# O's store and the modulation weights on GpSimd's DMA queue, and a reordered last stage, in a forward-and-backward memory transformer block

## The chip, the cores and the metric

The kernel runs on one core of a Trainium2 chip. The metric is the device time of one execution in microseconds (us); lower is better. The core has five engines with an instruction stream each: TensorE (PE; its weight loads are listed as PEld), VectorE (DVE), ScalarE (ACT), GpSimd (POOL) and SyncE (SP, which here only issues DMAs; its instructions appear as SPq). DMAs are issued by SP, GpSimd and in places ACT, and all of them are carried by the core's 16 DMA engines.

## The reference

The reference computes the output of a transformer block and the gradients of all its inputs. The block is a normalised attention with a recurrent memory, followed by a gated linear unit (GLU), each with shift, scale and gate rows that come from `silu(c) @ w_mod`. Cut to what matters here:

```python
mod = (_silu(c) @ w_mod).reshape(c.shape[0], 6, 1, -1)      # sa, ca, ga, sb, cb, gb
mem = mem0
for s in range(n_seg):                                       # 64 segments of 32 rows
    h = jnp.concatenate([mem, xs], axis=1)                   # 8 memory rows and 32 rows
    q, k, v = (einsum('btd,dhe->bhte', h, W) for W in (Wq, Wk, Wv))   # 32 heads of 128
    p = _softmax(where(mask, einsum('bhqe,bhke->bhqk', q, k) * scale, -1e9))
    o = einsum('bhqk,bhke->bhqe', p, v)
    o = einsum('bhte,hed->btd', o, Wo)
    mem = o[:, :M, :].copy()                                 # the next segment's memory
    outs.append(o[:, M:, :])
x = x + ga * attention(layernorm(x) * (1 + ca) + sa)
h = layernorm(x) * (1 + cb) + sb
x = x + gb * ((sigmoid(h @ w_gate) * (h @ w_up)) @ w_down)
# and the vjp of all this with grad_out
```

The sequence has 2048 rows of 512, so there are 64 segments; the eight memory rows make each segment depend on the one before. The backward pass needs V, P (the normalised softmax), O per head before the output projection, Q and K of every segment, so the forward pass stores them in DRAM.

## The kernel before, in words

`phase2` is the forward attention. Its loop `for s in range(NS)` has one turn per segment, called a stage here; `s4 = s % 4` is its position in a group of four segments, which share 128 rows. Heads are packed three to a 128-wide column block, so there are G = 11 blocks, in parts of four, four and three.

A stage does this. `proj` multiplies the segment's rows by Wk and Wq (L257), `v_chunk` by Wv (L677). `turns` transposes K and Q on TensorE. `st_exp` forms the scores (L900) and ACT their exponentials into `ET` (L902). `den` and `recip` (L906, L911) give the reciprocals of the row sums, `rden`. `pv` multiplies by V (L926); `ost` scales the product by `rden` into `Ost`, one part on DVE (L957), one on ACT (L954), one on DVE. `ott_first` and `ott_rest` transpose `Ost` into `OT`, `outproj` multiplies by Wo (L223), and `split_pair` with `sum_pair` give the stage's result, whose first eight columns ACT copies into the next stage's `hT` (L1133). In `split_pair` DVE writes `at_lo` (L232) once a stage, which makes a handy stage mark.

Besides that chain each stage moves data out. On SP, in this order: a DMA transpose of V into `VTr` (L1051), a DMA transpose of the exponentials `ET` into `Pst` (L1059), the store of `Ost` to `OSR` (L1089), the store of `OT` (L1127), every fourth stage or so six stores of the tail rows of K or Q, in some stages a load of modulation weights (`mod_rest`, L195), then for the stage before the stores of `VTr` and `Pst` to `VT` and `PS` (L1154, L1155), and the stores of K and Q (`rows_out`, L608 and L609). On GpSimd: the scaling of `Pst` by `rden` (L1152), three DMAs that bring the tail rows of V (L847), copies of the tails of K and Q (L65), the stores of attention rows to `AOA` (L811, L347), the copy `ao_tail` (L2379), and the copy of the next-but-one stage's input rows into `hT` (L563). The scaling of `Pst` and the stores of `VTr` and `Pst` are one closure, `norm`, which is put into `norms` at the end of a stage and called in the next.

`mod_rest` makes the later modulation rows in 16 pieces of 128 columns: `load` fetches the weights of a piece, `products` (L200) multiplies them one stage later.

The order of the work is written out by hand: `self.pin(i0)` at the end of `phase2` ties every engine's instructions of this phase to the order of the program text, and with them the order of the DMAs in each issuing engine's queue. The tile framework adds the waits. DMAs issued by SP take eight semaphores in turn, those issued by GpSimd another eight, so a DMA also waits until the one eight places before it has landed. `Ost` and `Pst` have one buffer each; `ET`, `OT`, `Vst` and the projected rows `RA` have two.

The last stage (s = 63) differs. It already does the GLU's norm for the first 128 rows (`first_tile_steps`; its variance is raised to a power on GpSimd, L776, and applied on DVE, L779). It transposes V and P on TensorE (`turn_v`, `turn_p`) and scales P by `rden` itself (`scale_p`, L946). It issues the loads of the next phase: rows for the GLU's second tile (`glu_load(1)`), `w_gate` (L996), `w_up` (L1061) and `w_down` (L1086), which take over the memory of Wk and Wv once these have been read.

`phase3` is the GLU, forward and backward, over 16 tiles of 128 rows. For the first tile PE multiplies by `w_gate` (L1333) and `w_up` (L1337), transposes `w_down` (L1242), and later needs `hhT`, a DMA transpose of the gated product `hh` (L1341) issued by SP (L1357, used in L1379). DVE prepares the second tile's rows meanwhile (L1266 to L1292).

Of the kernel before, what the change touches and what calls it, by code (L numbers as in the profile page):

```python
# [9 lines left out]
AF = mybir.ActivationFunctionType  # L10
ALU = mybir.AluOpType
# [29 lines left out]
class K:  # L41
# [145 lines left out]
    def mod_rest(self, psp, pool, k):  # L187

        nc, D, DC = self.nc, self.cfg.D, self.cfg.DC
        sl = slice(2 * D + 128 * k, 2 * D + 128 * k + 128)  # L190
        st = {}

        def load():
            st["w"] = pool.tile([128, DC, 128], BF16, name="wmod_r", bufs=1)
            nc.sync.dma_start(st["w"][:], self.io["w_mod"].rearrange("(cc p) n -> p cc n", p=128)[:, :, sl])  # L195

        def products():
            ps = psp.tile([128, 128], F32, name="mod_ps", tag="p")
            for n in range(2 * DC):
                nc.tensor.matmul(ps[0:32, :], lhsT=self.sc_keep[n % 2][:, n // 2, :], rhs=st["w"][:, n // 2, :],  # L200
                                 start=(n == 0), stop=(n == 2 * DC - 1))

            def put():
                row = pool.tile([1, 128], F32, name="modrow", bufs=1)
                nc.scalar.activation(row[:], ps[0:1, :], AF.Copy)
                nc.gpsimd.dma_start(self.MODROW[:, sl], row[:])

            return put

        return load, products  # L210
# [238 lines left out]
    def phase2(self):  # L449
        nc, tc, cfg, io = self.nc, self.tc, self.cfg, self.io  # L450
        D, DC, H, E, L, M, T, G, NS = cfg.D, cfg.DC, cfg.H, cfg.E, cfg.L, cfg.M, cfg.T, cfg.G, cfg.NS
        GW = 128
        NP = 3
        PG = 4
# [10 lines left out]
        with ExitStack() as ctx:  # L465
# [30 lines left out]
            Vsts = ptiles("Vst", 2)  # L496
            Ost = ptiles("Ost", 1)[0]
# [78 lines left out]
            def gl3(t):  # L576
                return t[:, :].rearrange("p (g x) -> p g x", x=GW)

            def x120(t, g):
                return t[:, g * 120:g * 120 + 128]  # L580
# [224 lines left out]
            norms = []  # L805
# [11 lines left out]
            turned_p = {}  # L817
# [39 lines left out]
            for s in range(NS):  # L857
# [13 lines left out]
                QT, KT, Vst, ET, OT = XT["q"], XT["k"], Vsts[s % 2], ETs[s % 2], OTs[s % 2]  # L871
                RA = RAs[s % 2]
                rden = sb2.tile([120, G], F32, name="rden")
# [21 lines left out]
                def st_exp(pi):  # L895
                    st_ps = masked.pop(pi)
                    n = min(PG, G - pi * PG)
                    for j in range(n):
                        g = pi * PG + j
                        nc.tensor.matmul(st_ps[:, j, 0:120], lhsT=x120(KT, g), rhs=QT[:, g * 120:g * 120 + 120],  # L900
                                         start=False, stop=True, skip_group_check=True)
                    nc.scalar.activation(part3(ET, pi)[:, 0:n, 0:120], st_ps[:, 0:n, 0:120], AF.Exp, scale=cfg.scale)  # L902
# [33 lines left out]
                def turn_p(pi):  # L936
                    n = min(PG, G - pi * PG)
                    ps = pst.tile([128, PG, GW], BF16, name="pt_ps", tag="st")
                    for j in range(n):
                        g = pi * PG + j  # L940
                        nc.tensor.transpose(ps[:, j, :], ET[:, g * GW:(g + 1) * GW], self.ident[:, :])
                    turned_p[pi] = ps

                def scale_p(pi):
                    n = min(PG, G - pi * PG)
                    nc.vector.tensor_tensor(Pst[0:120, pi * PG:pi * PG + n, :], turned_p[pi][0:120, 0:n, :],  # L946
                                            rden[:, pi * PG:pi * PG + n].unsqueeze(2).to_broadcast([120, n, 128]), op=ALU.mult)

                def ost(pi, or_ps, eng):
                    n = min(PG, G - pi * PG)  # L950
# [43 lines left out]
                if s == NS - 1:  # L994
                    self.glu_first = {1: self.glu_load(1, nc.sync)}
                    nc.gpsimd.dma_start(self.w_gate, io["B_w_gate"].rearrange("(c p) f -> p c f", p=128))  # L996
                    norms.pop()()
                if s == 0:
                    load_wo(3)
                    p1(P1_AHEAD, 0)  # L1000
# [35 lines left out]
                if s == NS - 1:  # L1036
                    v_chunk(s, 2)
                    first_tile[5]()
                st_exp(0)
                st_exp(1)  # L1040
                st_exp(2)
# [15 lines left out]
                if s < NS - 1:  # L1057
                    Pst = sb2.tile([128, G, 128], BF16, name="Pst", bufs=1)
                    nc.sync.dma_start(Pst[:], ET[:, :], transpose=True)  # L1059
                else:  # L1060
                    nc.gpsimd.dma_start(self.w_up, io["B_w_up"].rearrange("(c p) f -> p c f", p=128))  # L1061
                or1 = pv(1)
                ost(0, or0, "dve")
                ost(1, or1, "act")
# [18 lines left out]
                    self.pop_later()  # L1083
                self.pop_later()
                if s == NS - 1:
                    nc.gpsimd.dma_start(self.w_down, io["B_w_down"].rearrange("(fc p) d -> p fc d", p=128))  # L1086
                    for g0, t, w in ((0, RAs[0]["k"], 8), (8, RAs[0]["q"], G - 8)):
                        nc.sync.dma_start(self.VT[s, :, g0:g0 + w, :], t[:, 0:w * GW].rearrange("p (g x) -> p g x", x=GW))
                nc.sync.dma_start(self.OSR[s], gl3(Ost))  # L1089
                at_ps = outproj()  # L1090
                if s == NS - 1:
                    nc.sync.dma_start(self.OT[s], gl3(OT))
                    tail.collect(s4, [OT])
                    tail.begin(s - nseg_t + 1, [Wo])
                    first_tile[6]()
                    nc.scalar.activation(self.first_st[:, 11:12], self.first_st[:, 10:11], AF.Sigmoid)
                    parts = self.split_pair(sb2, at_ps, "at")
                    while tail.pieces:
                        tail.chunk()
                    tail.between = lambda: turn_p(0)  # L1100
                    tail.split()
                    first_tile[8]()
                    first_tile[7]()
                    ft = self.sum_pair(psp, parts, "at", "p")
                    self.store_rows(psp, sb2, ft, self.AOA[s + 1, 0:32, :], "at", "p")
                    self.pop_later()
                    self.pop_later()
                    turn_p(1)
                    self.pop_later()
                    for pi in (2, 0, 1):  # L1110
                        scale_p(pi)
                    break
                evac_turned()
                if s in first_tile[0]:
# [30 lines left out]
                    tail.collect(s4, [OT])  # L1145
                tail.split()
                self.store_rows(psp, sb2, ft, self.AOA[s + 1, 0:32, :], "at", "p")
                if s4 == nseg_t - 1:
                    tail.begin(s - nseg_t + 1, [Wo])

# [6 lines left out]
                if s < NS - 1:  # L1157
                    norms.append(norm)
            self.glu_first[0] = self.glu_load(0, nc.sync)
            nc.sync.dma_start(self.PS[NS - 1], Pst[:])  # L1160
            late_rows()
            self.pinned = self.pin(i0)

# [1357 lines left out]
```

## Time and profile before

| what | value |
|---|---|
| median of 3 runs | 2974.27 us |
| lowest and highest | 2969.84, 2976.05 us |
| profiled execution | 2976.26 us |
| its span | 2974.5 us |
| granted TensorE clock, mean | 0.998 |
| PE busy | 2913.0 us (98%) |
| DMA queue q1 (issued by SP and ACT) | 485.29 MB, 66.3% of the engines' time |
| DMA queue q0 (issued by GpSimd) | 148.63 MB, 15.9% |

The span runs from the first to the last instruction of the profiled execution; 1.76 us lie around it. A busy share is an average over phases: the forward loop takes the first 948 us, the GLU runs to about 1460 us, the attention's backward loop to about 2420 us, and weight gradients fill the rest. In the timeline a line gives start, length, engine, line of the kernel, operation and tiles, and in brackets the idle time before it with what ended it.

### The profile page before, as it was taken

Reading aid. Unit: us, or ns where it says so; the run is one execution under the profiler, and the core shown is the slowest. Engines: PE = TensorE matmul, PEld = TensorE weight load, DVE = VectorE, ACT = ScalarE, POOL = GpSimd, SP = SyncE. Lnnn points to the kernel's source line nnn. Section 1 sums busy time; section 2 is a strip of 40 time slices with the busy share of each in tenths; the row PEclk is TensorE's granted clock in tenths of the full one; section 3 lists DMA queues with packets and bytes.
Section 4 is the critical chain, followed back from the end, with each engine's and each line's share of the span. In section 5 each row is a group of like instructions: output and inputs, shape, how many; then the busy total and the mean of one; then the engine's idle time right before and its main releaser. Section 6 shows DMA issues by size and latency. Waiting matters only on the chain.

```text
span 2974.5 us, 105438 instructions
## 1 busy us (share of the span) xinstructions
PE 2913.0 (98%) x43838; PEld 1818.8 (61%) x43838; DVE 1625.0 (55%) x3689; ACT 1340.7 (45%) x3234; POOL 1231.7 (41%) x2487
## 2 busy tenths in 40 slices
PE   6999999999998999999999999999999999999999
PEld 3666666666665444445677776777777754445545
DVE  5565565665555788733456665666566632850011
ACT  3666666666665444312355555555555520110011
POOL 2555555545545222221344444444444432762111
PEclk9999999999999999999999999999999999999999
DMA  9889988998899899998699999999999997786565
GB/s 308 221 226 220 219 220 223 219 216 220 211 228 275 210 231 229 239 284 276 193 248 259 246 255 238 253 250 253 252 253 253 250 278 245 250 265 191 161 215 172
DMA packets 838066, 703.01 MB, mean 236 GB/s; under 512 B 537698, under 2 KB 710162, under 8 KB 836692
## 3 DMA queue, kind: packets, MB, share of 16 engines
q1 hardware_dynamic: 711972, 485.29, 66.3%
q0 software_dynamic: 54512, 148.63, 15.9%
q10 hardware_dynamic: 71104, 62.34, 6.5%
q8 instruction: 345, 5.65, 0.8%
q14 instruction: 133, 1.09, 0.1%
HBM read 294.99 MB, written 276.35 MB: 192 GB/s over the span
## 4 chain that ended last, share of the span: by engine, by line
PE 88%; DMA 4%; issue 3%; DVE 2%; ACT 1%; POOL 1%; SPq 0%; DVEq 0%; POOLq 0%; ACTq 0%
PE gps L2300 14%; PE pass_ps L257 14%; PE dh_ps L215 8%; PE g_ps L1923 5%; PE pass_ps L677 5%; PE gps5o L2315 4%; PE dhq_ps L223 4%; PE at_ps L223 4%; PE dh_tps L215 3%; PE gps L1583 3%; PE mm L1404 2%; PE turn_ps L890 2%; PE tps L1840 2%; PE st_ps L900 1%; PE mm L1364 1%
## 5 line engine op out<-in xcount | busy, mean ns | idle before, releaser
L2300 PE MATMUL gps<-rows,hrows 128*128 128x512 bf16 (+2 forms) x2160 | 415.5, 355 | 0.0
L2300 PEld LDWEIGHTS <-hrows 128*128 128x128 bf16 x2160 | 211.1, 98 | 204.5 <-issue 0.9
L1152 POOL TENSOR_TENSOR Pst<-Pst,rden 120x1408 bf16<-120x1408 bf16 x63 | 159.7, 2535 | 344.5 <-issue 209.0
L63 DVE CAST ot<-gps 128x512 bf16<-128x512 f32 (+3 forms) x76 | 48.1, 633 | 308.2 <-PE gps L2300 222.5
L1968 POOL COPY dOst<-RAd 96x512 bf16<-96x512 bf16 x128 | 75.1, 611 | 298.9 <-DVE RAd L63 298.7
L61 ACT ACTIVATE ot<-gps 128x512 bf16<-128x512 f32 (+3 forms) x75 | 41.2, 549 | 348.2 <-PE gps L2300 220.1
L677 PE MATMUL pass_ps<-Wv,hT 128*32 128x512 bf16 (+2 forms) x2304 | 186.8, 357 | 0.0
L2304 POOL DMA_DIRECT2D out_dram<-ot x104 | 78.6, 756 | 255.8 <-DVE ot L63 129.5
L257 PEld LDWEIGHTS <-hT 128*32 128x32 bf16 x4096 | 117.2, 97 | 95.9 <-issue 5.7
L63 DVE CAST Vst<-pass_ps 96x512 bf16<-96x512 f32 x128 | 87.3, 682 | 106.2 <-ACT RBv L61 102.7
L215 PE MATMUL dh_ps<-WvT,dVT 128*32 128x512 bf16 x2048 | 134.5, 383 | 1.7 <-DVE RBd L63 0.2
L223 PE MATMUL at_ps<-Wo,OT 128*32 128x256 bf16 x4096 | 128.1, 276 | 1.3 <-DMA Wo<-in_A_Wo_dram 0.9
L677 PE MATMUL pass_ps<-Wv,hb 128*32 128x512 bf16 (+2 forms) x636 | 126.5, 339 | 0.2
L257 PE MATMUL pass_ps<-Wk,hT 128*32 128x512 bf16 x2048 | 122.7, 380 | 2.1 <-POOL hT L563 1.1
L257 PE MATMUL pass_ps<-WoT,dyT 128*32 128x256 bf16 (+1 forms) x3072 | 122.8, 308 | 1.0 <-ACT dyT L2049 0.9
L257 PE MATMUL pass_ps<-Wq,hT 128*32 128x512 bf16 x2048 | 123.2, 379 | 0.3 <-DVE RBk L63 0.3
L223 PE MATMUL dhq_ps<-WqT,dQT 128*32 128x256 bf16 x4096 | 123.1, 273 | 0.2 <-issue 0.2
L215 PE MATMUL dh_ps<-WkT,dKT 128*32 128x512 bf16 x2048 | 122.3, 380 | 0.0
L2315 PE MATMUL gps5o<-WoT,rows 128*128 128x512 bf16 x560 | 121.0, 379 | 0.0
L223 PEld LDWEIGHTS <-dQT 128*32 128x32 bf16 x4096 | 109.9, 97 | 16.1 <-issue 0.4
L317 DVE TENSOR_TENSOR dST<-dh_ps,dST 128x512 bf16<-128x512 f32 x64 | 44.3, 692 | 130.3 <-ACT dST L316 130.3
L1910 DVE SCALAR_TENSOR_TENSOR dS<-dp_ps,Pst_l 128x480 bf16<-128x480 f32 (+1 forms) x192 | 106.2, 608 | 12.4 <-PE dp_ps L1908 6.7
(480 smaller groups left out, 7040.3 us busy)
## 6 DMA issues: line engine op xcount, KB each, us to landing
OSR<-Ost SPq DMA_DIRECT2D x64, 352.0 KB
OT<-OT SPq DMA_DIRECT2D x64, 352.0 KB
PS<-Pst SPq DMA_DIRECT2D x64, 352.0 KB
Pst_l<-PS SPq DMA_DIRECT2D x64, 352.0 KB
OT_l<-OT SPq DMA_DIRECT2D x64, 352.0 KB
DVR<-rows_x POOLq DMA_DIRECT2D x64, 352.0 KB, 6.0
DKR<-rows_x POOLq DMA_DIRECT2D x64, 352.0 KB, 5.7
DQR<-rows_x POOLq DMA_DIRECT2D x64, 352.0 KB, 3.5
```

Of the source, the lines that this page charges most:

```text
L63: return nc.vector.tensor_copy(out, in_)
L215: self.nc.tensor.matmul(ps[32 * j:32 * j + 32, :], lhsT=lhsT, rhs=w, start=(n < 4), stop=(n >= total - 4), tile_position=(0, 32 * j))
L223: nc.tensor.matmul(ps[32 * j:32 * j + 32, :], lhsT=x[k], rhs=w[k][:, 256 * d:256 * d + 256], start=(n == 0), stop=(n == total - 1), tile_p ...
L257: self.nc.tensor.matmul(ps[32 * j:32 * j + 32, :], lhsT=lhs(c), rhs=rhs, start=(c == 0), stop=(c == DC - 1), tile_position=(0, 32 * j))
L677: nc.tensor.matmul(ps[32 * j:32 * j + 32, o * E:(o + n) * E], lhsT=lhsT, rhs=wc[:, 3 * a + hl:3 * (a + n - 1) + hl + 1:3, :], start=(c == ...
L1152: nc.gpsimd.tensor_tensor(Pst[0:120, :, :], Pst[0:120, :, :], rden[:, :].unsqueeze(2).to_broadcast([120, G, 128]), op=ALU.mult)
L1583: nc.tensor.matmul(ps[:], lhsT=h2r[:, j, c * 128:(c + 1) * 128], rhs=xr[:, j, :], start=(j == 0), stop=(j == NT - 1))
L1910: nc.vector.scalar_tensor_tensor(out=part3(dS, pi)[:, :, 0:120], in0=ps[:, 0:n, 0:120], scalar=cfg.scale, in1=part3(Pst, pi)[:, :, 0:120], ...
L1923: nc.tensor.matmul(ps[:, j, 0:w], lhsT=lh[:, g * GW:(g + 1) * GW], rhs=rh[:, g * GW:g * GW + w], start=True, stop=True)
L2300: nc.tensor.matmul(ps[:, 0:ng * E], lhsT=hrows[:, tp_, c * 128:(c + 1) * 128], rhs=rows[:, tp_, 0:ng * E], start=(tp_ == 0), stop=(tp_ == ...
L2304: (nc.sync if i == len(todo) - 1 else nc.gpsimd).dma_start(outw[c * 128:(c + 1) * 128, h0:h0 + 3 * (ng - 1) + 1:3, :], ot[:, 0:ng * E].rea ...
L2315: nc.tensor.matmul(pss[gg][:], lhsT=rows[:, t, gg * E:(gg + 1) * E], rhs=dyrows[:, t, :], start=(n == 0), stop=(n == NTP - 1))
```

## The change

Four things are changed, all in `phase2` and `mod_rest`.

The store of `Ost` moves in stages 0 to 62 from SP's queue, ahead of the output projection, to GpSimd's queue, behind the calls that fold and store the stage's result. In stage 63 it stays on SP, and is now issued behind the projection's products in the program text.

The load of a piece of modulation weights moves from SP's queue to GpSimd's.

In stage 63 the closure `norm` of stage 62 moves from behind the projections of K to behind the norm's statistics, so that on GpSimd the scaling of P comes after the power L776. `w_up` is loaded right behind `w_gate`, and `w_down` ahead of `norm`.

In stage 63 `scale_p` runs on ACT, in eleven instructions of 128 columns in place of three on DVE, and writes into `Vst`, which is free by then, not into `Pst`. The three parts are spread over the end of the stage, and the store to `PS` reads `Vst`.

```diff
@@ mod_rest
-            nc.sync.dma_start(st["w"][:], self.io["w_mod"].rearrange("(cc p) n -> p cc n", p=128)[:, :, sl])
+            nc.gpsimd.dma_start(st["w"][:], self.io["w_mod"].rearrange("(cc p) n -> p cc n", p=128)[:, :, sl])
@@ scale_p
-                    n = min(PG, G - pi * PG)
-                    nc.vector.tensor_tensor(Pst[0:120, pi * PG:pi * PG + n, :], turned_p[pi][0:120, 0:n, :],
-                                            rden[:, pi * PG:pi * PG + n].unsqueeze(2).to_broadcast([120, n, 128]), op=ALU.mult)
+                    for j in range(min(PG, G - pi * PG)):
+                        g = pi * PG + j
+                        nc.scalar.activation(Vst[0:120, g * GW:(g + 1) * GW], turned_p[pi][0:120, j, :], AF.Copy,
+                                             scale=rden[:, g:g + 1])
@@ stage 63, behind the projections of K
                     nc.gpsimd.dma_start(self.w_gate, io["B_w_gate"].rearrange("(c p) f -> p c f", p=128))
-                    norms.pop()()
+                    nc.gpsimd.dma_start(self.w_up, io["B_w_up"].rearrange("(c p) f -> p c f", p=128))
@@ stage 63, behind the last part of V
                     first_tile[5]()
+                    nc.gpsimd.dma_start(self.w_down, io["B_w_down"].rearrange("(fc p) d -> p fc d", p=128))
+                    norms.pop()()
@@ between the products with V
-                else:
-                    nc.gpsimd.dma_start(self.w_up, io["B_w_up"].rearrange("(c p) f -> p c f", p=128))
@@ ahead of the output projection
                 if s == NS - 1:
-                    nc.gpsimd.dma_start(self.w_down, io["B_w_down"].rearrange("(fc p) d -> p fc d", p=128))
...
-                nc.sync.dma_start(self.OSR[s], gl3(Ost))
                 at_ps = outproj()
                 if s == NS - 1:
+                    nc.sync.dma_start(self.OSR[s], gl3(Ost))
                     nc.sync.dma_start(self.OT[s], gl3(OT))
...
                     parts = self.split_pair(sb2, at_ps, "at")
+                    scale_p(2)
...
                     self.pop_later()
+                    scale_p(0)
                     self.pop_later()
                     turn_p(1)
+                    scale_p(1)
                     self.pop_later()
-                    for pi in (2, 0, 1):
-                        scale_p(pi)
                     break
@@ end of the other stages
                 self.store_rows(psp, sb2, ft, self.AOA[s + 1, 0:32, :], "at", "p")
+                nc.gpsimd.dma_start(self.OSR[s], gl3(Ost))
@@ behind the loop
-            nc.sync.dma_start(self.PS[NS - 1], Pst[:])
+            nc.sync.dma_start(self.PS[NS - 1], gl3(Vsts[(NS - 1) % 2]))
```

## The prediction

> **What bounds the kernel now.** I read the page first: engine shares, the DMA row, the chain by line.
>
> ```profile
> span 2974.5 us, 105438 instructions
> PE 2913.0 (98%) x43838; PEld 1818.8 (61%) x43838; DVE 1625.0 (55%) x3689; ACT 1340.7 (45%) x3234; POOL 1231.7 (41%) x2487
> DMA  9889988998899899998699999999999997786565
> ...
> PE 88%; DMA 4%; issue 3%; DVE 2%; ACT 1%; POOL 1%; SPq 0%; DVEq 0%; POOLq 0%; ACTq 0%
> ```
>
> TensorE carries 88% of the chain, and the DMA engines are nine tenths busy through the first third (the loop over 64 stages, to about 948 us). The change touches only that loop and its end, so what it can win is the time in which PE waits there. The tile view of `Ost` says how much waits for its store to `OSR`:
>
> ```profile
> L1089 SPq DMA_DIRECT2D OSR<-Ost x64: 350/804/1962, 62.4 to 944.9; - x64
> ...
>   DMA OSR<-Ost: 10.7, 12
> ```
>
> `Ost` has one buffer, so the next stage's scaling (L957 on DVE, L954 on ACT) waits until the store has landed. Stage length I took as the distance between starts of `at_lo` (L232, once a stage): 13.96 to 14.03 us by stage position, and stages 1 to 62 together exceed that by 7.0 us. In the timeline DVE's first scaling starts 0.09 us after the reciprocal (L911) in an undisturbed stage; in stages 1, 4, 9, 13, 22, 28, 44, 47, 51, 52 it starts 0.74, 0.78, 0.41, 0.28, 0.44, 0.40, 0.29, 0.67, 0.53, 1.36 us after it: 5.9 less 10 x 0.09, so 5.0 us of the 7.0.
>
> The timeline of one stage shows where the two queues stand when `Ost` is ready (474.69 + 0.56 = 475.25):
>
> ```profile
> 480.13 0.39 POOL L2379 COPY ao_tail<-OT 128x264 bf16<-128x264 bf16 x1
> 480.48 0.26 POOL L563 COPY hT<-hx 128x96 bf16<-128x96 bf16 x1
> ...
> 483.89 0.53 SPq L1089 DMA_DIRECT2D OSR<-Ost  x1
> ```
>
> SP comes to the store at 483.89, behind two DMA transposes. GpSimd would come to it just ahead of the `hT` copy, at 480.48; the next `Ost` write is at 487.93. Last, the timeline of stage 63 and after, engine by engine:
>
> ```profile
> 936.74 2.53 POOL L1152 TENSOR_TENSOR Pst<-Pst,rden 120x1408 bf16<-120x1408 bf16 x1 [3.90 <-issue]
> 939.24 0.57 POOL L776 TENSOR_TENSOR st<-st 128x1 f32<-128x1 f32 x1
> ...
> 939.85 0.55 DVE L779 TENSOR_SCALAR RBv<-x,st 128x512 f32<-128x512 f32 x1 [2.36 <-POOL st L776]
> ...
> 942.15 1.14 ACT L954 ACTIVATE Ost<-or_ps,rden 120x128 bf16<-120x128 f32 x4 [2.89 <-DMA OSR<-Ost]
> ...
> 953.31 1.75 DVE L946 TENSOR_TENSOR Pst<-pt_ps,rden 120x384 bf16<-120x384 bf16 x3 [1.22 <-DMA PS<-Pst]
> ...
> 959.49 0.96 PE L1242 MATMUL tp<-ident,Wv 128*128 128x128 bf16 x14 [1.13 <-DMA Wv<-in_B_w_down_dram]
> ...
> 977.75 0.75 PE L1379 MATMUL mm<-Wv,hhT 128*128 128x512 bf16 x2 [3.08 <-DMA hhT<-hh]
> ```
>
> Stage 63 takes 18.95 us (929.15 to 948.11). Two things hold it at once: the power (L776) stands on GpSimd behind P's scaling (L1152), and stage 62's `OSR` store lands at 942.04. Then come three DMA-made waits.
>
> **The change part by part.** All sums are against the profiled execution, 2976.26 us (span 2974.5, 1.76 around it). The three runs' median is 2974.27, 2 us lower, which is as much as the waits vary from run to run.
>
> *O's store, 63 times, from SP to GpSimd.* SP loses 0.80 us a stage; OT, VT, PS and the K and Q stores behind it come earlier, but nothing on the path waits for those, so this counts nothing. GpSimd gains an issue of 0.57 us (the 352 KB store of `DVR` has that row). Behind it stand the `hT` copy (used a stage later), P's scaling, V's tail rows and the K and Q tails; cover is GpSimd's idle time before P's scaling, 324 us over 59 stages in the waits view. So the cost of the issue is nothing. What matters is whether the store lands before the next `Ost` write. From the start of each stage's `hT` copy to that write there are 6.83 us or more at the last position of each group of four, 7.45 to 7.54 typically at the first and third, 9.6 at the second; stages 22 and 44 are outliers with 5.53 and 4.61, where P came late. The landing of such a store from GpSimd is not in the trace for the forward loop. The nearest rows are the same size in the backward loop:
>
> ```profile
> DMA to landing us min/median/max: 2.8/3.5/4.9
> DMA to landing us min/median/max: 4.6/5.7/7.4
> DMA to landing us min/median/max: 4.7/6.0/8.3
> ```
>
> (`DQR`, `DKR`, `DVR`.) With one landing time for all 62 stages, the lateness adds up to 0 at 3.5, 0.4 at 5.0, 1.9 at 6.0, 9.5 at 7.3 and 32.5 at 8.0. I take 5.0, the mean of the three medians, since 128 KB stores from GpSimd in this very loop (`H1ROWS`) land in 4.3 and SP's own 352 KB store in stage 51 landed 4.5 after its issue (779.71 to 784.2). Result: -5.0 + 0.4 = -4.6 (bounds -5.0 and +27). [...]
>
> *Modulation weights, 16 loads, from SP to GpSimd.* Two loads come too late now: PE waits at L200 in stages 7 and 55, and periods 8 and 56 are 0.39 and 0.48 us long. Issued on GpSimd a few us sooner and used a stage later, both waits go: -0.9. The issue costs GpSimd 0.5 to 0.8 (`MODROW` 0.51; `w_gate`, with as many runs, 0.78), ahead of O's store at the third position, where 7.45 shrinks to about 6.7; still over 5.0, so nothing.
>
> *Last stage, the power ahead of P's scaling, stage 62's store sooner.* The variance is ready at 934.80; the power is done by 935.5 and DVE's L779 follows the V copy at 937.5. The copies of V and the reciprocal then end near 939.45, not 941.18. O's store of stage 62 goes out at 932.1 ahead of `w_gate` in the same queue and is there by 938 if it takes 5.0 to 6.0. `Ost` starts at 939.5, not 942.15: 2.65. PE's idle stretches at 939.4 to 942.9 mostly go, and with them the clock of 0.50 and 0.66 that the windows show at 944 to 948, where L223's 64 products took 3.46 instead of 1.94 us: up to 1.4 more. At `at_lo` stage 63 is then 4.0 shorter. P's scaling now ends about 942.3; behind it wait the store of `at_rb` and the `ao_tail` copy, needed by PE at 944.8: 1 us of slack.
>
> *GLU weights sooner, P of stage 63 on ACT.* The 4.0 meet the transfers:
>
> ```profile
> 934.00:936.00 2.00, 2.00 (x34) 1.26 (x31) 1.60 (x5) 1.19 (x3) 0.00 (x0) 1.00 0.97 291
> 942.00:944.00 2.00, 1.04 (x12) 0.69 (x12) 1.80 (x5) 1.14 (x4) 0.00 (x0) 0.99 0.95 234
> 954.00:956.00 2.00, 2.00 (x13) 1.05 (x11) 1.97 (x4) 1.48 (x3) 0.66 (x3) 1.00 1.04 408
> ```
>
> The last two columns are DMA share and GB/s: full from 930 to 960, with a dip at 942 to 944, when `w_gate` is in and `w_up` (issued 941.08, landed 11.7 later) only starts. Issued at 933 and 939, the weights leave no such gap; at some 270 KB a us (`w_gate`, 1.8 MB, went at that rate from 934 to 940), O's store and 5.5 MB end near 957, not 959.4. So PE's L1242 moves by 2 to 2.5, not 4.0. DVE loses 1.75 us and a 1.22 us wait, ACT gets 11 scalings of 0.285 (1.14 for four in L954): three in its 1.34 us of idleness before L316, eight in the 2.18 before the first sigmoid; 0.2 to 0.5 may stick out, which the wait for `w_up` covers. New wait: P of stage 63 lies in `Vst`, whose memory the first `hh` (L1341) takes over, so `hh` waits for that store. It went out at 956.86, `hh` ran at 963.68; with a landing of 4.4 to 10.1 (P's store of stage 62, issued 943.08, took the latter) this costs 0 to 3.3 after a shift of 2.5; I take 0, as the queue is emptier by then (0.76 share at 960 to 965). After that PE waits 3.08 for `hhT`, whose transpose SP issues at 969.60, 8.8 us after OT's landing released its queue (960.76). If SP's queue is released as much sooner as the weights land, the wait stays as it is; if not sooner at all, the gain shrinks to under 1; if 5 sooner, the wait goes too. Ends 0.5 and 5.1; I take 2.7, near the weights' shift.
>
> Sum: -4.6 - 0.9 - 2.7 = -8.2, so 2968.1, rounded 2968.0.
>
> **The rivals.**
>
> *O's store lands late (slower).* If behind the two transposes a store from GpSimd needs 8.0 us, 43 of 62 stages are stalled: 32.5 - 5.0 - 0.9 - 2.7 = +23.9, 3000. It decides from a landing of 7.3 on. For it: `DVR` reaches 8.3, and stage 62's store on SP took 9.7 beside `w_gate`. Against: no median above 6.0, and GpSimd's queue has only small stores at that moment.
>
> *The queue changes, the transfers do not (no change).* The engines are 0.9 busy whoever issues. If O's store pushes the transposes of P back by its own time, P's scaling, the next item on GpSimd, goes back too and with it the next store: the loop gives some 2, the tail 0.5, in all -2 to -4: 2972 to 2974. For it: P's scaling waits for its transpose in most stages, and two stages have little slack already. [...]
>
> *The tail opens fully.* SP's queue drained 5 us sooner, `hhT` no longer waited for: -5.1 in place of -2.7, with the loop at its best 2965, down to 2962.
>
> **How the numbers follow.** Forecast 0.50, open tail 0.10, no change 0.24, late store 0.16. A measurement of this kernel tells about 0.2%, 6 us, from no change, so the forecast (6.3 under the median) lies just beyond it: of its 0.50 I count 0.40 as faster. Faster 0.50, same 0.10 + 0.24 = 0.34, slower 0.16. The range runs from the open tail, 2962, to just past the median with one or two stages stalled more, 2979; it leaves out the late store and little else. The forecast's own range is 2964 to 2972.
>
> **What would show it.** Right: the lengths of stages 1 to 62 exceeding undisturbed ones by under 2 us in all, not 7.0; no wait for `OSR` over 1 us in all; no PE wait for `wmod_r`; stage 63 at 15 us; L776 before L1152 on GpSimd; `w_down`'s end near 957. Wrong: `OSR<-Ost` landing over 7 us after its issue on GpSimd; DVE and ACT waiting for it at the last position of every group; `hh` waiting for `PS<-Vst`; the wait for `hhT` grown to 5.

## The result, and the profile after

The changed kernel is slower. Its median is 3025.59 us against 2971.42 us for the kernel before, a ratio of the medians of 1.018. The comparison's own ratio is 1.0107, 95% interval [1.0079, 1.0135]; it counts only executions within 1.5% of the changed kernel's fastest, and since these spread from 2976 to 3046 us, most are left out of it, the profiled one too; `e2` below shows the same loss with none left out. The prediction was 2968.0 us, range 2962 to 2979. The profiled execution took 3029.94 us.

The page of the changed kernel, the lines that answer to the first fence of the prediction:

```profile
span 3028.2 us, 105299 instructions
PE 2932.9 (97%) x43838; PEld 1821.5 (60%) x43838; DVE 1628.0 (54%) x3686; ACT 1343.6 (44%) x3245; POOL 1286.9 (42%) x2566
DMA  9888888888899989998699999999999997786565
...
PE 65%; DMA 2%; issue 2%; DVE 1%; ACT 1%; POOL 0%; SPq 0%; DVEq 0%; POOLq 0%; ACTq 0%
```

TensorE does the same work, but is busy 19.9 us longer, and the span is 53.7 us longer. The chain is no help here: it could be followed back only to 877.5 us, so it covers little of the loop. The starts of `at_lo` do. The one of stage 62 has moved from 929.15 to 983.35, so the loop lost 54.2 us; from there to the end it is 2044.8 us against 2045.3. The loss is not spread evenly. By position in the group of four, the median stage is 13.96, 14.03, 16.36 and 15.47 us (before 13.98, 14.02, 13.96 and 14.01): the third is longer, and often the fourth.

What stands in the third position is shown by the tile view of `b_colsk`, the tile from which GpSimd copies the last rows of K (`kT`, L65) in every stage, and which ACT fills anew once in four stages:

```profile
L65 POOL COPY kT<-b_colsk x186: 187/230/812, 68.6 to 983.9; 128x192 bf16<-128x192 bf16 x62, 128x48 bf16<-128x48 bf16 x62, 128x16 bf16<-128x16 bf16 x62
L61 ACT ACTIVATE b_colsk<-turn_ps x15: 597/597/603, 83.4 to 924.9; 128x512 bf16<-128x512 bf16 x15
...
who waited for it (us, times):
...
  ACT b_colsk L61: 37.5, 13
```

ACT waited 37.5 us for GpSimd's copies, in 13 stages. The same line of the kernel before:

```profile
  ACT b_colsk L61: 1.0, 2
```

Stage 18, in the timeline of the changed kernel, SP, GpSimd, ACT and PE in turn (start, duration, and in brackets the idle time before it and what ended it):

```profile
311.60 1.85 SPq L1054 DMA_TRANSPOSE VTr<-Vst  x1
313.54 2.23 SPq L1062 DMA_TRANSPOSE Pst<-ET  x1
322.31 0.42 SPq L1156 DMA_DIRECT2D VT<-VTr  x1
322.92 1.95 SPq L1157 DMA_DIRECT2D PS<-Pst  x1
...
311.67 0.56 POOL L1149 DMA_DIRECT2D OSR<-Ost  x1
312.22 0.28 POOL L563 COPY hT<-hx 128x96 bf16<-128x96 bf16 x1
320.36 2.54 POOL L1154 TENSOR_TENSOR Pst<-Pst,rden 120x1408 bf16<-120x1408 bf16 x1 [7.87 <-DMA Pst<-ET]
324.42 0.65 POOL L65 COPY kT<-b_colsk 128x192 bf16<-128x192 bf16 x3
...
325.10 0.60 ACT L61 ACTIVATE b_colsk<-turn_ps 128x512 bf16<-128x512 bf16 x1 [3.46 <-POOL kT L65]
325.59 0.38 ACT L230 ACTIVATE at_hi<-at_ps 128x256 bf16<-128x256 f32 x1
...
326.02 0.27 PE L242 MATMUL at_ft<-foldsel,at_hi 128*128 128x32 bf16 x4 [2.56 <-ACT at_hi L230]
```

O's store is issued 0.07 us after the transpose of V starts on SP. P's transpose, issued at 313.54, lets P's scaling start only at 320.36; the copies `kT` stand behind the scaling, ACT's `b_colsk` behind the copies, and `at_hi`, for which TensorE waits, behind that. In the kernel before, P's scaling started 6.84 us after `at_lo` of stage 17 (302.37 less 295.53) in this stage; here 11.25 us after it (320.36 less 309.11), and the stage takes 16.96 us.

The fourth position is explained by the row of Wk's products in the page and by the granted clock. The row, before and after:

```profile
L257 PE MATMUL pass_ps<-Wk,hT 128*32 128x512 bf16 x2048 | 122.7, 380 | 2.1 <-POOL hT L563 1.1
...
L257 PE MATMUL pass_ps<-Wk,hT 128*32 128x512 bf16 x2048 | 135.0, 409 | 2.1 <-POOL hT L563 1.1
```

That is 12.3 us more for the same 2048 products, 409 ns each instead of 380. Windows of 1 us around the stall of stage 18 (window, length, busy time and instructions of PE, PEld, DVE, ACT and POOL, then granted clock, DMA share, GB/s):

```profile
323.00:324.00 1.00, 0.46 (x12) 0.00 (x0) 0.00 (x0) 0.00 (x0) 1.00 (x3) 1.00 0.94 345
324.00:325.00 1.00, 0.00 (x0) 0.00 (x0) 0.00 (x0) 0.00 (x0) 1.00 (x4) 1.00 0.61 169
327.00:328.00 1.00, 1.00 (x20) 0.56 (x16) 0.93 (x5) 1.00 (x4) 1.00 (x3) 0.50 0.70 217
328.00:329.00 1.00, 1.00 (x16) 0.46 (x12) 0.46 (x2) 0.31 (x2) 0.98 (x3) 0.50 0.80 203
329.00:330.00 1.00, 1.00 (x16) 0.33 (x12) 0.45 (x1) 0.00 (x0) 1.00 (x3) 0.50 1.17 125
330.00:331.00 1.00, 1.00 (x24) 0.44 (x20) 0.24 (x1) 0.25 (x1) 0.68 (x2) 0.98 1.18 161
```

After the idle stretch TensorE's granted clock is 0.81 in the window at 326, 0.50 in the three from 327 and 0.98 at 330. So 36.5 us of added waiting for `b_colsk` and 12.3 us of slower products make up 48.8 of the 54.2, as a rough account: a wait of ACT need not delay TensorE by as much.

The waits for O's store, which the change was expected to remove, have nearly doubled. The tile view of `Ost`, from which the prediction had 10.7 us in 12 waits of DVE and ACT together, now has:

```profile
  DMA OSR<-Ost: 20.2, 14
```

Of these 10.7 us are DVE's, in seven stages (4.5 in five before). The tile view of `OSR`, changed kernel:

```profile
L1149 POOL DMA_DIRECT2D OSR<-Ost x63: 542/557/607, 56.5 to 988.1; - x63
...
  DVE Ost L958: 10.7, 7
...
DMA to landing us min/median/max: 3.5/5.4/9.3
```

And the last stage (timeline of the changed kernel, GpSimd, then DVE, then PE):

```profile
990.72 0.57 POOL L776 TENSOR_TENSOR st<-st 128x1 f32<-128x1 f32 x1 [0.54 <-DVE st L775]
996.45 2.53 POOL L1154 TENSOR_TENSOR Pst<-Pst,rden 120x1408 bf16<-120x1408 bf16 x1 [0.81 <-issue]
...
997.41 2.13 DVE L783 SCALAR_TENSOR_TENSOR RBv<-ca_bc,RBv 128x512 f32<-128x512 f32 x1
...
1013.75 0.96 PE L1244 MATMUL tp<-ident,Wv 128*128 128x128 bf16 x14 [0.24 <-DMA Wv<-in_B_w_down_dram]
1032.66 0.60 PE L1381 MATMUL mm<-Wv,hhT 128*128 128x512 bf16 x2 [3.98 <-DMA hhT<-hh]
```

The power (L776) is ahead of the scaling, and stage 63 is 17.10 us long instead of 18.95. But `w_down` is used 30.4 us after `at_lo` of stage 62, as before (30.3), and the wait for `hhT` is 3.98 us, not 3.08.

### The profile page after: what moved, and what is told of

It reads as the page before. It is cut to its first block, busy times and chain, and to the rows that moved or that the text cites. A ratio compares the mean times of both kernels' runs of the same rounds, so it can differ in the third digit from the quotient of the medians.

```text
span 3028.2 us, 105299 instructions
## 1 busy us (share of the span) xinstructions
PE 2932.9 (97%) x43838; PEld 1821.5 (60%) x43838; DVE 1628.0 (54%) x3686; ACT 1343.6 (44%) x3245; POOL 1286.9 (42%) x2566
## 3 DMA queue, kind: packets, MB, share of 16 engines
q14 instruction: 132, 1.08, 0.1%
## 4 chain that ended last, share of the span: by engine, by line
PE 65%; DMA 2%; issue 2%; DVE 1%; ACT 1%; POOL 0%; SPq 0%; DVEq 0%; POOLq 0%; ACTq 0%
PE gps L2302 14%; PE dh_ps L215 8%; PE pass_ps L257 6%; PE g_ps L1925 5%; PE gps5o L2317 4%; PE dhq_ps L223 4%; PE mm L1406 3%; PE dh_tps L215 3%; PE gps L1585 2%; PE mm L1381 2%; PE mm L1366 2%; PE tps L1842 1%; PE mm L1335 1%; PE mm L1339 1%; PE gps L1484 1%
## 5 line engine op out<-in xcount | busy, mean ns | idle before, releaser
L1154 POOL TENSOR_TENSOR Pst<-Pst,rden 120x1408 bf16<-120x1408 bf16 x63 | 159.8, 2536 | 392.4 <-issue 284.3
L257 PE MATMUL pass_ps<-Wk,hT 128*32 128x512 bf16 x2048 | 135.0, 409 | 2.1 <-POOL hT L563 1.1
```

Of the source, the lines that this page charges most:

```text
L257: self.nc.tensor.matmul(ps[32 * j:32 * j + 32, :], lhsT=lhs(c), rhs=rhs, start=(c == 0), stop=(c == DC - 1), tile_position=(0, 32 * j))
L1154: nc.gpsimd.tensor_tensor(Pst[0:120, :, :], Pst[0:120, :, :], rden[:, :].unsqueeze(2).to_broadcast([120, G, 128]), op=ALU.mult)
```

## The theories

Theory A: P goes round a loop once a stage. SP issues the DMA transpose of P; when it has landed GpSimd scales P; when that is done SP issues P's store; behind it in SP's queue stand K's and Q's stores and the next two transposes, so the next transpose of P cannot be issued earlier. In the kernel before, O's store stood behind both transposes in the same queue. From GpSimd it is under way beside them, P lands later, and the loop becomes longer than a stage; what depends on GpSimd then falls behind until it stops the path. Theory B: GpSimd's own additional instructions delay its queue. Theory C: the rebuilt last stage costs the time.

The loop can be measured in each profiled execution: means over stages 2 to 61, worked out from the starts and ends in the timelines, in us. The last column says how long after `at_lo` P's scaling starts.

| kernel | P's transpose issued to scaling | scaling | to P's store | store to next transpose of P | sum | scaling after `at_lo` |
|---|---|---|---|---|---|---|
| before | 4.97 | 2.54 | 0.68 | 5.85 | 14.04 | 7.74 |
| after | 6.41 | 2.54 | 0.12 | 5.92 | 14.99 | 10.11 |
| `e1` store back on SP | 5.12 | 2.54 | 0.49 | 5.98 | 14.13 | 7.82 |
| `e2` store alone | 6.05 | 2.54 | 0.29 | 6.05 | 14.93 | 10.22 |
| `e6` idle instructions | 5.07 | 2.54 | 0.57 | 5.86 | 14.04 | 7.17 |
| `e9` half the store | 5.70 | 2.54 | 0.34 | 5.99 | 14.57 | 9.61 |
| `e10` store between | 4.96 | 2.54 | 0.37 | 6.78 | 14.64 | 9.99 |
| `e8` tails first | 6.26 | 2.54 | 0.32 | 5.78 | 14.89 | 12.60 |
| `e12` less scaling | 5.87 | 1.26 | 0.81 | 6.16 | 14.09 | 5.18 |
| `e11` after, P before V | 6.44 | 2.54 | 0.92 | 4.03 | 13.94 | 4.04 |
| `e13` before, P before V | 5.83 | 2.54 | 1.54 | 4.03 | 13.94 | 2.57 |
| `e14` `e13` and the store | 6.14 | 2.54 | 1.25 | 4.33 | 14.26 | 7.90 |

The sum is within 0.12 us of the mean stage, as it must be when both go in step (from the `at_lo` starts of stages 2 to 62, 14.09 before and 14.98 after), so the sum alone does not tell which of the two sets the pace. The column "to P's store" tells more: it holds SP's delay in coming to that store, and this is the slack. Before, it was 0.68 us a stage, 0.12 after. In the three kernels with P's transpose ahead of V's it is not all slack, because V's store stands ahead of P's on SP and waits there for V's transpose (46.0 us in 30 stages in `e13`).

## The experiments

### Which part: `e1` to `e4`

`e1_store_back`: the changed kernel, O's store returned to SP.

```
-                nc.gpsimd.dma_start(self.OSR[s], gl3(Ost))      # behind store_rows
+                nc.sync.dma_start(self.OSR[s], gl3(Ost))        # ahead of outproj()
```

> The changed kernel with O's store issued by SP again; the modulation weights and the last stage stay as changed. Theory A (in GpSimd's ring the store's transfer runs beside the two DMA transposes, they land later, and the loop transpose of P -> P's scaling on GpSimd -> store of P -> next transposes, about 14.0 us long before, becomes longer than a stage): the start of P's scaling returns from 15.0 us apart to 14.1, at_lo of stage 62 from 983 to below 931 us, and the time is 2964 to 2971 us. Theory B (GpSimd's own extra instructions, the modulation weights' loads among them, delay its queue): most of what came in the stages that load weights stays, 2975 to 2990 us. Theory C (the rebuilt last stage costs the time): no change to 3020 us or more.

2977.2 us, ratio to the kernel before 1.0005 [0.9995, 1.0015]. The loss is gone, and `b_colsk` waits 1.3 us in all. The level is a miss (2964 to 2971 was expected): the remaining two parts do not make the kernel faster than before.

`e2_store_alone`: the kernel before, with that one edit the other way round.

> The kernel before with O's store alone moved to GpSimd. Theory A: nearly the whole loss, 3015 to 3040 us, P's scaling 15.0 us apart. Theory C: as before, 2971 us. Theory B leaves room for less than theory A: 2990 to 3020 us.

3036.4 us, 1.0206 [1.0186, 1.0226]. One moved instruction brings the whole loss. ACT's wait (tile view of `b_colsk`, this kernel):

```profile
who waited for it (us, times):
  DVE b_colsk L63: 61.6, 15
  ACT b_colsk L61: 43.8, 15
```

`e3_weights_alone`: the kernel before with the modulation weights' loads on GpSimd.

```
-            nc.sync.dma_start(st["w"][:], self.io["w_mod"]...)
+            nc.gpsimd.dma_start(st["w"][:], self.io["w_mod"]...)
```

> The kernel before with the modulation weights' loads alone moved to GpSimd. Theory A: 2968 to 2973 us, no stage longer than before by more than 1 us. Theory B (GpSimd's queue is delayed by more issues): 2980 us or more, with the longer stages behind the loads at the third position of each group of four.

2981.4 us, 1.0025 [1.0013, 1.0038]. That is the level of theory B (2980 or more) and not of theory A, but without theory B's pattern: the third positions keep their normal length (13.96 us in the median). PE no longer waits for `wmod_r`, but stage 4 takes 18.91 us, 4.9 too long, and `Ost` waits 3.11 us for O's store there; no other stage exceeds its normal length by more than 1.6 us.

`e4_last_stage_alone`: the kernel before with the edits of stage 63 only (the power and the GLU weights ahead of P's scaling, P of stage 63 scaled by ACT into `Vst`).

> The kernel before with the edits of the last stage alone. The prediction's sum for this part is -2.7 us (bounds -0.5 and -5.1): 2968.7 us against 2971.4. Theory C: 3000 us or more.

2976.7 us, 1.0005 [0.9993, 1.0016]. Theory C falls, and the predicted -2.7 is not there. Stage 63 takes 19.15 us: with O's store still on SP, that of stage 62 holds it (timeline, DVE):

```profile
945.96 0.69 DVE L958 TENSOR_TENSOR Ost<-or_ps,rden 120x512 bf16<-120x512 f32 x1 [2.84 <-DMA OSR<-Ost]
```

### The issue or the transfer: `e6`, `e7`, `e9`, `e10`

`e6_idle_on_gpsimd`: the kernel before with idle instructions where the change issues the store.

```
                 self.store_rows(psp, sb2, ft, self.AOA[s + 1, 0:32, :], "at", "p")
+                for _ in range(2):
+                    nc.gpsimd.memset(idle_t[:], 0.0)
```

> The kernel before (O's store on SP) with two memsets of a scratch tile of 128x384 bf16 on GpSimd at the place where the change puts the store; a 128x264 copy there takes 0.39 us, so some 0.8 us in all, more than the store's issue of 0.56. Theory A (the transfer beside the transposes does it): 2970 to 2978 us, and b_colsk waits on ACT for the tail copies kT less than 4 us in all (1.0 before, 37.5 after the change). Theory B (GpSimd's queue is delayed by the instruction itself): 2995 us or more, with 15 us or more of that wait.

2975.1 us, 0.9997 [0.9984, 1.0009], and a wait for `b_colsk` of 2.1 us. The tile view shows what GpSimd was given in addition, 0.84 us a stage:

```profile
L1150 POOL MEMSET idle_t<- x126: 407/418/582, 56.4 to 935.3; 128x384 bf16 x126
```

Theory B falls.

`e7_store_act`: the kernel before, the store issued by ScalarE at its old place.

```
-                nc.sync.dma_start(self.OSR[s], gl3(Ost))
+                nc.scalar.dma_start(self.OSR[s], gl3(Ost))
```

> The kernel before with O's store issued by ScalarE at its old place in the program: the transfer leaves SP's queue and runs beside the two transposes, and GpSimd issues nothing more. Theory A: 3000 to 3040 us, P's scaling 14.6 us apart or more, b_colsk waits for kT's tail copies 25 us or more. Theory B: 2968 to 2980 us, that wait under 4 us.

3024.1 us, 1.0171 [1.0144, 1.0199]. The time and the loop (14.74 us) are as theory A has them, but the wait is not: 0.4 us for `kT`. The timeline of ACT shows another obstacle:

```profile
379.99 0.35 ACTq L1089 DMA_DIRECT2D OSR<-Ost  x1
380.39 0.60 ACT L61 ACTIVATE b_colsk<-turn_ps 128x512 bf16<-128x512 bf16 x1 [1.89 <-DMA VT<-VTr]
```

The store's issue on ACT waits until the store of V has landed, and that hangs on the same loop. So ACT is stopped by the issue itself, and this run does not separate the theories cleanly.

`e9_half_store`: the changed kernel, the store in two parts.

```
+                if s < NS - 1:
+                    nc.sync.dma_start(self.OSR[s, :, 6:G, :], gl3(Ost)[:, 6:G, :])
                 at_ps = outproj()
...
-                nc.gpsimd.dma_start(self.OSR[s], gl3(Ost))
+                nc.gpsimd.dma_start(self.OSR[s, :, 0:6, :], gl3(Ost)[:, 0:6, :])
```

> The changed kernel with O's store in two parts: six of the eleven column groups from GpSimd, five from SP at the old place. Theory A: about half of the loss, as the time that the transposes share is halved, 2980 to 3010 us, P's scaling 14.2 to 14.7 us apart. Theory B (the number of GpSimd's instructions counts, and it is the same as in the change): 3015 us or more.

3005.5 us, 1.0104 [1.0074, 1.0135]. With none, half or all of the store on GpSimd, P's transpose takes 4.97, 5.70 and 6.05 to 6.41 us to the scaling, and the loop 14.04, 14.57 and 14.93 to 14.99: it is the transfer that counts, and more of it costs more. GpSimd issues as many instructions as in the changed kernel.

`e10_store_between`: the kernel before, nothing on GpSimd, the store between the transposes in SP's queue.

```
                 nc.sync.dma_start(VTr[:], Vst[:, :], transpose=True)
...
                 nc.sync.dma_start(self.OSR[s], gl3(Ost))
+                if s < NS - 1:
+                    Pst = sb2.tile([128, G, 128], BF16, name="Pst", bufs=1)
+                    nc.sync.dma_start(Pst[:], ET[:, :], transpose=True)
```

> The kernel before with the three transfers in SP's queue in another order: transpose of V, O's store, transpose of P (before: transposes first, then the store). Nothing is moved to another queue. If it is the second ring that hurts (two rings in flight at once): no change, 2968 to 2980 us. If any place of the store that is not behind P's transpose lengthens the loop (the store's 0.80 us of issue and its transfer come between): P's scaling 14.4 us apart or more and 2990 us or more.

3012.1 us, 1.0127 [1.0108, 1.0145]. A second queue is not needed for the loss, nor an instruction on GpSimd: a place between the transposes is enough. Here P's transpose lands as fast as before (4.96 us) but is issued 0.93 us later in the loop. One stage in SP's timeline:

```profile
605.39 1.29 SPq L1051 DMA_TRANSPOSE VTr<-Vst  x1
606.78 0.83 SPq L1086 DMA_DIRECT2D OSR<-Ost  x1
607.66 1.45 SPq L1089 DMA_TRANSPOSE Pst<-ET  x1
```

### The one wait or the loop: `e8`, `e12`, `e11`, `e13`

`e8_tails_first`: the changed kernel; in the third position the norm is issued behind the tail copies.

```
-                if s < NS - 1 and norms:
+                if s < NS - 1 and norms and s4 != 2:
                     norms.pop()()
...
                         tails_in("kq", s + 1)
+                if s4 == 2:
+                    norms.pop()()
```

> The changed kernel with the norm (P's scaling on GpSimd and the stores of V and P) issued behind the tail copies of K and Q in the third stage of each group of four, so that ACT's b_colsk there no longer stands behind the scaling. If the loss enters the path only at that wait (37.5 of 52 us by the trace): 2968 to 2990 us, the wait under 4 us. If the loop through the transpose, the scaling and the store of P is itself longer than a stage (15.0 against 14.0 us): the stall comes up in another place and the time stays at 3010 us or more.

3047.2 us, 1.0231 [1.0202, 1.0260]. The wait for `b_colsk` falls from 37.5 to 2.6 us and nothing is won. The stall has moved, above all to `Ost` (tile view, what its engines sat idle for):

```profile
its engine sat idle before it (us, times) until:
...
  DMA OSR<-Ost: 58.2, 37
```

Of these 30.4 us are DVE's and 27.8 ACT's, mostly at the same time. The loop is still 14.89 us, so `b_colsk` was only the place where it stopped the path.

`e12_half_scaling`: the changed kernel, P's scaling cut to five of eleven column groups, so that six of them stay unscaled.

```
-                    nc.gpsimd.tensor_tensor(Pst[0:120, :, :], Pst[0:120, :, :],
+                    nc.gpsimd.tensor_tensor(Pst[0:120, 0:5, :], Pst[0:120, 0:5, :],
```

> The changed kernel with P's scaling on GpSimd cut to five of the eleven column groups; six stay unscaled, so this part of the computation is left out. The scaling falls from 2.54 to some 1.2 us; the store and its transfer stay. Theory A (the loop of 15.0 us falls to 13.7, under a stage): 2965 to 2985 us. If the transfer hurts in another way than through the loop: 3015 us or more.

2978.6 us, 1.0017 [0.9999, 1.0034]. Taking 1.28 us out of the loop recovers nearly all of the loss, with O's store left where the change put it.

`e11_p_before_v` and `e13_before_p_before_v`: the changed kernel and the kernel before with SP's two transposes swapped.

```
                 if s < NS - 1:
+                    Pst = sb2.tile([128, G, 128], BF16, name="Pst", bufs=1)
+                    nc.sync.dma_start(Pst[:], ET[:, :], transpose=True)
                     nc.sync.dma_start(VTr[:], Vst[:, :], transpose=True)
```

> The changed kernel with SP's two transposes swapped: P's first, then V's. The loop loses the time from V's transpose to P's, 2.25 us of 15.01 in the changed kernel, and would be some 12.8 us, shorter than a stage. Theory A (the loop sets the stage): the loss goes, 2962 to 2980 us, b_colsk waits for kT's tail copies under 4 us. If the loop is not the cause: 3015 us or more.

> The kernel before with SP's two transposes swapped. Its loop has 0.68 us of slack already, so theory A gives little: 2962 to 2976 us, from the waits in single stages where P came late. If the transpose of V becomes the late one: 2985 us or more.

`e11` took 2972.0 us, 1.0002 [0.9987, 1.0018], `e13` 2964.6 us, 0.9969 [0.9957, 0.9982]. The swap gives back all that the change lost, and it makes the kernel before 9 us faster. GpSimd's idle time ahead of P's scaling, from which the prediction took its cover, tells why; the page's row in the kernel before and in the changed one:

```profile
L1152 POOL TENSOR_TENSOR Pst<-Pst,rden 120x1408 bf16<-120x1408 bf16 x63 | 159.7, 2535 | 344.5 <-issue 209.0
...
L1154 POOL TENSOR_TENSOR Pst<-Pst,rden 120x1408 bf16<-120x1408 bf16 x63 | 159.8, 2536 | 392.4 <-issue 284.3
```

in `e11`, with the same instructions:

```profile
L1153 POOL TENSOR_TENSOR Pst<-Pst,rden 120x1408 bf16<-120x1408 bf16 x63 | 160.2, 2542 | 75.2 <-issue 61.8
```

and in `e13`:

```profile
L1151 POOL TENSOR_TENSOR Pst<-Pst,rden 120x1408 bf16<-120x1408 bf16 x63 | 159.9, 2538 | 38.5 <-issue 21.0
```

With the loop shorter than a stage P is there before GpSimd comes to it. DVE then waits for O's store 1.8 us in two stages, in `e13` and in `e11` alike, whichever queue the store is in; stages 1 to 62 of `e13` exceed the normal length by 3.1 us instead of some 7; and stage 63 takes 14.98 us instead of 18.95 without any edit in it. A P that comes in time is what it needs, and the swap is not the only way to that: in the profiled execution of `e6`, which has no swap, the scaling of stage 62's P happened to start 4.03 us after `at_lo` of that stage instead of 7.59, and stage 63 took 14.99.

### What the three parts are worth beside a short loop: `e14`, `e15`, `e16`

Each is `e13` with one part of the change.

> The kernel before with SP's transposes swapped and O's store on GpSimd, nothing else. The swap alone gave 2964.6 us. The prediction's term for the store (-4.6) would make it 2960. If the waits for O's store were a result of the late P (with the swap alone they are 3.2 us in all), the move gives nothing: 2963 to 2967 us. If the store in GpSimd's ring costs also without the loop: 2970 us or more.

> The kernel before with SP's transposes swapped and the edits of the last stage, nothing else. The prediction's -2.7 us would make it 2961.9. With the swap the last stage is already down from 18.95 to 14.98 us, so the power ahead of P's scaling has nothing to gain there: 2963 to 2967 us. If the edits cost: 2970 us or more.

> The kernel before with SP's transposes swapped and the modulation weights' loads on GpSimd, nothing else. The prediction's -0.9 us would make it 2963.7. If the loads cost what they did alone without the swap (0.25% of 2974, 7 us), and make up the difference between 2972 and 2964.6: 2970 to 2974 us.

`e14`, the store: 2983.8 us, 1.0026 [1.0005, 1.0047], executions from 2965 to 2998. It was expected at 2963 to 2967 if the loop were all, and at 2970 or more if the moved store costs beside a shortened loop too; it does, 19 us against `e13`. In the profiled execution the loop was at its limit again, 14.26 us, and GpSimd stood idle over 0.3 us before P's scaling in all 60 stages (16 in `e13`, 17 in `e11`). `e11` has the same store and the same swap and a loop of 13.94. One link that differs is the wait of P's transpose for the landing of P's store, which frees the single `Pst` (waits of SP in `e14`: us in total, times, longest):

```profile
SPq L1052 <- DMA PS<-Pst: 32.8, 39, 2.0
```

It is 17.8 in `e13` and 23.5 in `e11`. The wait of V's store for V's transpose does not tell them apart: 58.1 us in `e14`, but 63.6 in `e11`. Why one execution stays early and another late is open, and so is why `e11`, with more of the change in it, is faster than `e14`.

`e15`, the last stage: 2963.5 us, 0.9962 [0.9948, 0.9977], not to be told from `e13`. `e16`, the weights: 2968.3 us, 0.9979 [0.9968, 0.9991], between its two expectations; stage 3 takes 17.41 us, again with `Ost` late (timeline, DVE):

```profile
95.82 0.69 DVE L957 TENSOR_TENSOR Ost<-or_ps,rden 120x512 bf16<-120x512 f32 x1 [2.43 <-DMA OSR<-Ost]
```

That accounts for some 3 of the 3.7 us between `e16` and `e13` in one execution; the intervals overlap, so the rest is open. The best time is the kernel before with the swap, with or without the last stage's edits.

## Why the prediction was wrong

*"SP loses 0.80 us a stage ... nothing on the path waits for those, so this counts nothing."* This is the step that failed: what the moved transfer does to those beside it was put at nothing. What stood behind O's store on SP gained nothing (from P's store to the next transpose it is 5.92 us, before 5.85); the two transposes ahead of it, which my list of items left out, lost. From issue to scaling P's transpose went from 4.97 to 6.41 us (6.05 with the store alone moved, `e2`), against 0.68 of slack. P's round became 14.99 us long, and the forward loop lost 54.2 us where I had forecast a gain of 4.6 from this part.

*"GpSimd's idle time before P's scaling, 324 us over 59 stages" as cover.* For the issue it was cover, as I said: 0.84 us a stage of added work on GpSimd cost nothing (`e6`). My omission was to read it as room and not to see what ends it. GpSimd was waiting for a transfer that is itself released, round a loop, by GpSimd's scaling; against a later landing of that transfer such time covers nothing, and it grows with the loop, from 344.5 to 392.4 us by the page's rows. The slack was 0.68 us a stage, on SP, and I had not worked out the sum around the loop.

*O's store lands after 5.0 us: -5.0 + 0.4.* The landing was near (median 5.4), the wait was not: DVE waits 10.7 us in seven stages, and 1.8 us in two when the loop is short (`e11`, and `e13` with the store on SP): most of those waits come from the loop, not from the store's queue. With one part at a time the term is +2.06% of the kernel before, 61 us (`e2`), or 19 us beside the swap (`e14` against `e13`), in place of -4.6.

*The rival "the queue changes, the transfers do not".* It named the mechanism, P pushed back by the store's own time and the loop with it, and priced it at -2 instead of following it: a loop longer than a stage costs its excess in every stage, 0.89 us (14.98 less 14.09) x 62, or 55. The runs show that the moved store is not free for what it runs beside: from issue to scaling P's transpose took 0.73 us longer with half of it on GpSimd (`e9`), 1.1 to 1.4 with all of it (`e2`, the changed kernel).

*The rival "O's store lands late".* It forecast 3000 us, and the time went that way, but by another mechanism: the median landing of 5.4 us did not reach the 7.3 from which it was to decide, and of the 23 landings that the trace shows three were later (8.0 to 9.3).

*Modulation weights, -0.9.* The PE waits did go. The cost was in the same place as the store's: alone 1.0025 [1.0013, 1.0038], with an `Ost` wait of 3.11 us in one stage.

*The last stage, -2.7 between 0.5 and 5.1.* Two of its steps can be checked by `e15` against `e13`, whose loops are equal (times from `at_lo` of stage 62). The GLU weights are used at 25.00 instead of 27.34, 2.3 sooner as predicted. But the last P goes out later, and what stands behind its store on SP with it. From `e13`:

```profile
945.82 0.34 SPq L1159 DMA_DIRECT2D PS<-Pst  x1
```

and from `e15`, with the same start of the stage within 0.14 us:

```profile
950.10 0.34 SPq L1160 DMA_DIRECT2D PS<-Vst  x1
```

ACT's scaling is not what delays it: it ends at 944.61 in `e15`, DVE's at 945.79 in `e13`. The delay starts with the other edit. With `norm` behind the power, the scaling of stage 62's P starts 10.68 us after `at_lo` instead of 3.70, and SP waits for it before it issues that P's store (waits of SP in `e15`):

```profile
SPq L1155 <- POOL Pst L1152: 5.8, 1, 5.8
```

Stage 62's P goes out at 938.03 instead of 932.12, and all behind it in SP's queue goes later, the last P's store among it. So SP issues `hhT`'s transpose at 35.90, not 33.06, and PE gets `hhT` at 41.59 instead of 42.10: the gain shrinks to 0.5, the end that the prediction tied to SP's queue not being released sooner. No wait of `hh` for the last P's store shows in `e15`, so taking 0 there was right, but what the later `norm` does to SP's queue was not priced. By the end of the span it is gone (2036.30 against 2035.81). The store of stage 62 was correctly named as a second hold on stage 63: with the power moved and that store still on SP (`e4`) the stage stays at 19.15 us. In the changed kernel it is 17.10, not the 15 that was predicted; with the loop short it is 14.98 with the edits and without them (`e15`, `e13`).

## What to carry to other kernels

Before counting an engine's idle time as cover, see what ends it: if it is a transfer that the engine's own work releases one turn earlier, the time can take in more work of that engine (here 0.84 us a stage in `e6` at no cost), but not a later landing (here 1.08 us a stage in `e2`, for 61 us in all). Then add up the turn without its waits and compare it with the stage, because the difference is all the slack there is (0.68 us here). A transfer that leaves a queue also leaves its place behind other transfers, so list what it will run beside, not only what stood behind it. And where a loop is close to the stage, the order inside its queue is the cheap remedy: swapping two transposes was worth 9 us here, though it did not make the moved store free (`e14`).

## What the hardware showed that I had not expected

TensorE's granted clock fell after short stalls, but not after all of them. In stage 18 PE was idle from 323.47 to 326.02, 2.56 us, and the windows of 1 us above show 0.50 until 330. After stage 10, 2.4 us too long, stage 11 took the normal 14.00: PE had been idle for 1.93 us up to 204.76, and the windows from 205 to 222 show 1.00. In such windows the changed kernel's clock falls to 0.50 in ten stretches between the starts of `at_lo` of stages 1 and 62, that of the kernel before in none. The length of a stall alone does not tell which: the clock fell to 0.50, from 388 on, after one of 1.63 us that ended at 386.55, and it stayed at 1.00 in the windows from 85 to 91 after one of 2.00 us that ended at 84.79. What decides it, these runs do not show.

DVE's L783 (128x512, f32) took 2.13 us in the changed kernel, where GpSimd's scaling of P ran from 996.45 to 998.98 across it, and 0.68 us in `e4`, where GpSimd's scaling was over. In the kernel before it also took 0.68 us, and 1.41 in `e15`, where it ran from 937.15 to 938.56 and SP issued the store of the P scaled just before at 938.03.
